# Sums moved into TensorE's waits around the last mix, the last pair stored as two halves, and one load moved to another queue

## The chip, the cores and the metric

The kernel runs on one core of one Trainium2 chip. The metric is the device time of one execution in microseconds (us), taken over several executions. A profile shows one execution; its times start with the first instruction of the core.

The engines: PE is TensorE (PEld its weight loads), DVE is VectorE, ACT is ScalarE, POOL is GpSimd, SP is SyncE. A "q" behind an engine's name is its sequencer, which issues DMAs. GpSimd issues the large loads, SyncE the stores.

## The reference, cut to what matters

A linear attention (8 batches, 8 heads, 576 positions, head size 64) makes `x`. Then comes a spectral mix:

```python
X = np.fft.rfft(x, axis=1)                       # [... 64 of the modes kept]
Yr = einsum(Xr, w_r) - einsum(Xi, w_i)           # 64 modes, each 512 x 512, two weight sets
Yi = einsum(Xr, w_i) + einsum(Xi, w_r)
y = np.fft.irfft(Y, n=S, axis=1)
u = x + y
return u + np.maximum(u @ w_ch, 0.0)             # float32, 8 x 576 x 512
```

The weights `w_r` and `w_i` are 64 x 512 x 512 floats each, 134 MB together. They are read once, and they are most of the 163.64 MB that the profile shows read from HBM.

## The kernel before: the parts that the change and the argument touch

The weights go through SBUF in tiles of 8 modes. A `mix` multiplies one tile with the spectrum; the last mixes finish the modes 48 to 63 ("late" modes). All other modes have been added to `x` (in `xs`) and to its product with `w_ch` (in `xw`) before. What is left after the last mix is, for every chunk of 128 output rows, two sums in PSUM, `p` (which is u) and `q` (which is u @ w_ch):

```python
class Last:                           # one item: one chunk, or a pair of chunks
    def base(self, which):            # which=0: p <- turned xs;   which=1: q <- turned xw
        ...                           # single first items and pairs take p from banks(): 2 buffers
    def late(self, which):            # adds the late modes: rows of yl (y for p, z for q)
        r = 64 * a + 32 * which
        back(..., CL, yl, slice(r, r + 16 if self.early else r + 32), not self.early)
    def straight(self, which):        # only the first chunks ("early"): last 8 modes from yst, zst
        pe.matmul(..., lhsT=CM[:, n], rhs=(yst, zst)[which], start=False, stop=True)
    def relu(self): ...               # ACT: relu of q, into rl
    def store(self): ...              # DVE: p + rl, then a DMA by SyncE
```

The late sums of later items read 32 rows of `yl`. The upper 16 of them are copies of the results of the very last mix: `yst` (y) and `zst` (y @ w_ch). Four DMAs make these copies; the second copy of `zst` is issued by GpSimd:

```python
def put(src, o, dst, copies):
    if o < 6:
        sp.dma_start(dst[16 * o:16 * o + 16], src)
    else:
        for s in copies:
            r = 32 * s + 16 * (o - 6)
            (sp, pool)[s // 2 if o == 7 else 0].dma_start(yl[r:r + 16], src)
```

Around the last mix:

```python
if not mixq:
    seq[0].base(1); seq[0].late(1)             # before the last mix
mix(...)                                       # waits for the last weights
seq[0].base(0); seq[0].late(0)
# yst = py + yacc (DVE), transposes (PE), yT (ACT, DVE)
seq[0].straight(0); seq[0].keep_p(); seq[1].base(1)
# pz = yT @ w_ch (PE), zst = pz (ACT, DVE), put(zst, ...)
seq[1].late(1); seq[1].base(0); seq[1].late(0)
seq[0].straight(1); ...                        # needs zst
for g, s in enumerate(seq):                    # t is the next item
    # t.base(1), s.base(0), t.late(1), s.late(0), t.relu(), s.store()   [cut]
```

## Time and profile before

| what | number | where it is read |
|---|---|---|
| time before | 452.13 us median of 3 runs (451.09 to 453.21) | timed runs |
| span of the profiled run | 450.4 us | page |
| last weight tile: issue to landing | 375.78 to 414.22 us | chain of waits |
| last mix starts | 414.26 us | timeline |
| from there to the end | 36.1 us | 450.4 - 414.26 |
| one pair of chunks in the tail | PE 1.30, ACT 1.08, DVE 1.22 us | timeline |

The page's strip of the DMA engines shows how busy they are in 40 slices of the span, in tenths (9 is 90% or more):

```profile
DMA  8999999999999999999999999999999999995597
```

They are 90% busy or more in 36 of 40 slices. Most of the kernel is a stream of weights, and the compute is arranged around it. The chain of waits of the last 40 us of before follows (start us, us, what):

```profile
375.78 38.44 DMA wt<-in_moe_w_i_dram
...
414.26 0.67 PE pt L37 x8
414.93 0.64 PE pp L37 x2
...
442.06 1.24 DVE of L37
...
443.38 0.60 ACT rl L37
...
444.50 1.22 DVE of L37
```

The stream ends at 414.22, 38 us after the issue of its last tile: that is how long the queue is. Between `414.93` and `442.06` the chain holds nothing but PE, apart from three pieces of 0.05 us or less (cut here). The timeline of before shows the steps that matter (start us, us, engine, operation, out<-in, count, and in brackets the idle time before and its releaser):

```profile
414.26 0.67 PE L37 MATMUL pt<-wt,XT 128*32 128x512 bf16 x8 [1.43 <-DMA wt<-in_moe_w_i_dram]
414.87 0.39 PE L37 MATMUL pp<-xs,CF 128*128 128x512 bf16 x1
415.19 0.39 PE L37 MATMUL pp<-yl,CL 16*128 16x512 bf16 x1
...
417.47 0.43 DVE L37 CAST zst<-pt 128x256 bf16<-128x256 f32 x1 [1.07 <-PE pt L37]
...
418.27 0.39 PE L37 MATMUL pp<-zst,CF 128*128 128x512 bf16 x1
418.50 0.54 POOL L37 DMA_DIRECT2D yl<-zst  x1 [1.60 <-DVE zst L37]
...
422.03 0.39 PE L37 MATMUL pt<-yl,CL 32*128 32x512 bf16 x2
...
422.35 0.61 PE L37 MATMUL pt<-xw,CF 128*128 128x512 bf16 x2
```

PE idles 1.43 us before the last mix. The base and late sum of the first chunk stand right after it (414.87, 415.19). GpSimd issues its copy of `zst` at 418.50. The view of issues gives 3.5 us from issue to landing for it, so it lands at 422.0. PE comes to the first late sums over 32 rows at 422.03 and finds them ready.

At the head, the timeline of before shows what releases PE:

```profile
2.85 0.75 POOL L37 DMA_DIRECT2D vn<-in_v_dram  x1
...
8.01 0.49 DVE L37 CAST w2blk<-xs 64x128 bf16<-64x128 f32 x2
...
8.23 1.12 PE L37 MATMUL one<-ident_b,kb 128*128 128x128 bf16 x9 [8.23 <-DVE w2blk L37]
...
9.14 1.30 PE L37 MATMUL one<-ident_b,qb 128*128 128x128 bf16 x10
...
10.38 1.89 PE L37 MATMUL two<-w2blk,kT 128*128 128x256 bf16 x8
```

GpSimd spends 0.75 us on the issue of v, and DVE's tables wait for what GpSimd does after it.

### The profile page before, as it was taken

How to read it: one execution, taken by the hardware profiler on the slowest of the kernel's cores; microseconds unless marked ns; L12 is line 12 of the kernel's file. 1: busy time of each engine (PE TensorE's matmuls, PEld its weight loads, DVE VectorE, ACT ScalarE, POOL GpSimd, SP SyncE). 2: the span in 40 equal slices, each digit the busy share in tenths (PEclk: the TensorE clock that was granted, in tenths of full speed). 3: DMA queues.
4: the chain of work that ended last, by engine and by line, in shares of the span. 5: the costliest groups of instructions: out<-in, count | busy, mean ns of one | idle time of the engine just before them, and what ended most of it. 6: DMA issues, size and time to landing. Idle time of an engine off the chain costs nothing.

```text
span 450.4 us, 9754 instructions
## 1 busy us (share of the span) xinstructions
PE 329.1 (73%) x4069; PEld 209.5 (47%) x4113; DVE 276.3 (61%) x519; ACT 274.6 (61%) x472; POOL 94.8 (21%) x128
## 2 busy tenths in 40 slices
PE   2577658669678767778768769208998677898994
PEld 2355546547456545566546646103554333343331
DVE  6667675655777567577676677664333233776685
ACT  3588868665898687598777675032433222664673
POOL 7142132123131222232321112401312120000000
PEclk9979988886999699699998989757999999999998
DMA  8999999999999999999999999999999999995597
GB/s 162 233 207 207 234 208 234 232 208 261 207 207 234 234 234 232 213 230 227 217 230 225 229 218 206 206 207 207 209 207 220 214 215 214 202 201 100 195 380 314
DMA packets 83981, 99.27 MB, mean 220 GB/s; under 512 B 2464, under 2 KB 79136, under 8 KB 83936
## 3 DMA queue, kind: packets, MB, share of 16 engines
q0 software_dynamic: 78192, 86.78, 108.5%
q1 hardware_dynamic: 5744, 11.86, 8.1%
q8 instruction: 32, 0.52, 0.4%
q14 instruction: 13, 0.11, 0.1%
HBM read 163.64 MB, written 9.44 MB: 384 GB/s over the span
## 4 chain that ended last, share of the span: by engine, by line
DMA 28%; PE 26%; issue 17%; ACT 12%; DVE 12%; POOL 5%; ACTq 0%; POOLq 0%; DVEq 0%
DMA wt<-in_moe_w_i_dram 13%; PE pt L37 11%; PE one L37 8%; DMA wt<-in_moe_w_r_dram 8%; DMA vn<-in_v_dram 6%; ACT AB L37 5%; PE two L37 4%; DVE m L37 3%; POOL wt L37 3%; ACT AQ L37 3%; PE pp L37 3%; DVE mk L37 2%; DVE zall L37 2%; DVE va L37 1%; DVE xs L37 1%
## 5 line engine op out<-in xcount | busy, mean ns | idle before, releaser
L37 ACT ACTIVATE AB<-two 128x1024 bf16<-128x1024 f32 x64 | 62.8, 1051 | 8.1 <-DVE mk L37 6.7
L37 ACT ACTIVATE AQ<-two 128x1024 bf16<-128x1024 f32 x64 | 63.2, 1059 | 2.6 <-PE two L37 2.6
L37 ACT CAST xw<-pt 128x512 bf16<-128x512 f32 x50 | 29.4, 588 | 43.2 <-PE pt L37 43.2
L37 PE MATMUL pt<-wchb,xT 128*128 128x512 bf16 x127 | 36.3, 398 | 22.4 <-DVE xT L37 20.8
L37 DVE TENSOR_REDUCE m<-two 128x8 f32<-128x1024 f32 x32 | 39.2, 1224 | 19.9 <-PE two L37 19.8
L37 DVE TENSOR_REDUCE mk<-two 128x8 f32<-128x1024 f32 x32 | 39.0, 1221 | 15.2 <-PE two L37 14.7
L37 DVE TENSOR_TENSOR va<-vn,ee 128x1152 bf16<-128x1152 f32 x32 | 42.0, 1355 | 3.4 <-DMA vn<-in_v_dram 3.4
L37 POOL DMA_DIRECT2D wt<-in_moe_w_r_dram x30 | 26.5, 885 | 78.8 <-PE pt L37 47.9
L37 POOL DMA_DIRECT2D wt<-in_moe_w_i_dram x28 | 24.8, 887 | 67.0 <-PE one L37 33.6
L37 DVE RECIPROCAL rd<-one 128x6 f32<-128x6 f32 x48 | 9.4, 196 | 47.1 <-PE one L37 47.1
L37 ACT COPY kT<-one 128x512 bf16<-128x512 bf16 (+1 forms) x32 | 19.1, 641 | 27.0 <-PE one L37 26.9
L37 PEld LDWEIGHTS <-minus 96*128 96x128 bf16 x288 | 26.2, 109 | 19.5 <-issue 13.3
L37 PE MATMUL two<-w2blk,qT 128*128 128x256 bf16 x128 | 21.9, 299 | 16.5 <-ACT AB L37 12.3
L37 PEld LDWEIGHTS <-XT 128*32 128x32 bf16 x512 | 18.3, 179 | 31.7 <-issue 18.0
L37 PEld LDWEIGHTS <-xs 128*128 128x128 bf16 x304 | 24.5, 99 | 15.1 <-issue 8.1
L37 PE MATMUL two<-mT,minus 96*128 96x128 bf16 x256 | 28.6, 241 | 3.0 <-issue 1.7
L37 PEld LDWEIGHTS <-qT 128*128 128x128 bf16 x144 | 14.5, 104 | 31.0 <-issue 27.9
L37 PEld LDWEIGHTS <-xT 128*128 128x128 bf16 x144 | 13.4, 102 | 32.0 <-DVE xT L37 20.5
L37 DVE TENSOR_TENSOR xs<-one,rd 128x384 bf16<-128x384 f32 x48 | 26.8, 557 | 1.6
L37 DVE COPY xT<-pt 128x512 bf16<-128x512 bf16 x36 | 15.2, 422 | 19.9 <-PE pt L37 19.9
L37 PE MATMUL pt<-wt,XT 128*32 128x512 bf16 x208 | 18.5, 431 | 11.4 <-DMA wt<-in_moe_w_i_dram 8.7
L37 PE MATMUL one<-kvz,AQ 128*128 128x65 bf16 x512 | 26.6, 206 | 0.1
(129 smaller groups left out, 695.0 us busy)
## 6 DMA issues: line engine op xcount, KB each, us to landing
wt<-in_moe_w_r_dram POOLq DMA_DIRECT2D x30, 1024.0 KB, 25.3
wt<-in_moe_w_i_dram POOLq DMA_DIRECT2D x28, 1024.0 KB, 24.7
vn<-in_v_dram POOLq DMA_DIRECT2D x16, 576.0 KB, 18.4
out_dram<-of SPq DMA_DIRECT2D x17, 512.0 KB, 3.6
kb<-in_k_dram POOLq DMA_DIRECT2D x16, 288.0 KB, 19.7
qb<-in_q_dram POOLq DMA_DIRECT2D x16, 288.0 KB, 18.3
xs<-in_moe_w_i_dram POOLq DMA_DIRECT2D x2, 1024.0 KB, 25.3
yacc<-in_moe_w_r_dram POOLq DMA_DIRECT2D x1, 1024.0 KB, 9.8
```

Of the source, the lines that this page charges most:

```text
L37: ins = f(*args, **kwargs)
```

## The change

The intent has three parts. (a) SyncE issues v of the first unit, so GpSimd gets to its other work sooner. (b) Sums of the first chunks move into waits of PE: the first chunk's `p` goes before the last mix, the second chunk's sums move up one place, and the third item's base of `q` goes into the wait for `zst`. (c) The last pair becomes two single chunks, so that its first half is stored earlier.

```diff
-        def load_v(self):
+        def load_v(self, eng=pool):
-            load(self.vn, v, self.g, self.bp, pool)
+            load(self.vn, v, self.g, self.bp, eng)
-    units[0].load_v()
+    units[0].load_v(sp)                                                     # (a)
-    seq += [Last(*x) for x in pairs[3]]
+    seq += [Last(*x) for x in pairs[3][:3]] + [Last((3, 6)), Last((3, 7))]  # (c)
             seq[0].late(1)                                                  # (b), to the end
+            seq[0].base(0)
+            seq[0].late(0)
         mix(*key, wts.pop(key), XTb[g % 2], bank)
             if end:
-                seq[0].base(0)
-                seq[0].late(0)
+                seq[1].base(1)
+                seq[1].late(1)
                 seq[0].keep_p()
-                seq[1].base(1)
+                seq[1].base(0)
-    seq[1].late(1)
-    seq[1].base(0)
     seq[1].late(0)
+    seq[2].base(1)
     seq[0].straight(1)
-        if t:
+        if t and g > 1:
             t.base(1)
```

(The comments are added here, and lines between the pieces are cut.)

## The prediction

> **What bounds the kernel now.** A stream of weights, then a tail. In the windows table the DMA share is 1.20 to 1.26 (16 engines) in nearly every stretch from 4 to 407 us. The chain of waits has a piece "DMA wt<-in_moe_w_i_dram" from 375.78 to 414.22 us: the last weight tile lands 38 us after its issue, because the queue is full. TensorE does the last mix at 414.26, and 36 us of tail follow (to 450.4), in which the chain is nearly all PE: one pair of output chunks every 1.30 us, while DVE needs 1.23, ACT 1.09, and stores run at about 400 GB/s (512 KB in 1.30 us).
>
> **What the change does.**
> (a) v of the first unit goes by SyncE. GpSimd issues what follows 0.75 us earlier (v's issue took that at 2.85), so DVE's w2blk (8.01 to 8.50, which releases TensorE at 8.23) comes about 0.7 us earlier. But compute at the head is not the bound. What counts is how early the DMA engines fill: their share is 0.2 to 0.6 between 2.0 and 4.0 us, over 1.0 afterwards. SyncE has issued w_phi by 1.97; w_phi landed 2.9 us after issue, so v can flow from about 3.1 and use half of 0.7 us. The Trainium skill (DMA: Bandwidth & Descriptors, "Issuing engines are not separate DMA queues") says that several issuers save only sequencer time and share 16 engines; the full shares in the trace agree. Estimate: the stream ends 0.3 us earlier (0 to 0.7).
>
> (b) The first chunk's base and late sum (0.64 us of PE, 414.87 to 415.5) move into the wait for the last weights (412.85 to 414.26), so they are free. The same sums of the second chunk take their place, so transposes, yT and zst keep their times. After pz one late sum and two base sums (0.32 + 0.43) replace three sums that ended at 418.27; the first straight sum of z then starts at 418.07, bound by DVE's zst (417.90). PE is 0.2 us ahead, and 0.65 us once the third item's base sums are skipped.
> Most is lost at once: the first late sum that reads all 32 rows (PE at 422.03) needs the GpSimd copy yl<-zst, issued at 418.50 and landing 3.5 us later, about 422.0. Before, PE arrived just then; now it arrives near 421.4 and waits some 0.5 us. From there PE has no slack, so the tail keeps its times; only the first pair's store leaves 0.65 us earlier.
>
> (c) The last pair in halves: DVE 0.69 + 0.69 instead of 1.22. The last DVE operation was 444.50 to 445.72; store data flowed without a gap from 443.2 to 448.4 at 400 GB/s, so the last bytes move little: 0 to 0.3 us.
>
> **Sum.** 0.3 (head) + 0.1 (mix) + 0.15 (halves), about 0.6 us. Predicted 451.5 us, range 449.9 to 452.9 (three runs of before spread over 2.1 us). Faster by over 2%: 1%; within 2%: 98%; slower: 1%.
>
> **What would show it.** The last wt lands near 413.9; TensorE's first matmul comes near 7.5, not 8.23; the first chunk's base and late sum stand before the mix, which still waits for the DMA; a new PE wait on yl before the first 32-row late sum, about 0.5 us; the distance from last mix to end is shorter by 0.1 to 0.4 us, not 0.65; the last store's data end close behind the one before.
>
> **What would make it wrong.** The copy of zst lands earlier than I read, so the whole 0.65 us comes through; 2 KB store rows are slower; v on the other queue delays kb past 7.5 us; run-to-run spread hides everything.

## The result

The changed kernel took 452.34 us in the median of 6 runs (451.91 to 452.95). Before took 453.12 in the same rounds (451.09 to 453.71, 6 runs). The ratio is 0.9991, with a 95% interval of 0.9970 to 1.0013: the same, to within what the runs can tell. (A ratio is the mean time of one kernel's fast runs over that of the other's of the same rounds, so it is not quite the ratio of the medians.) A second set of rounds, after_again, gave 1.0001 (0.9976 to 1.0025).

In the profile the last mix starts at 413.42, which is 0.84 us earlier than in before. The end comes at 450.1, only 0.3 earlier. So the tail became longer: 36.7 us instead of 36.1. Most of that lies behind the landing of the last store; the section on why takes it up.

The timeline of the changed kernel around the last mix:

```profile
412.06 0.39 PE L37 MATMUL pp<-xs,CF 128*128 128x512 bf16 x1
...
412.38 0.38 PE L37 MATMUL pp<-yl,CL 16*128 16x512 bf16 x1
...
413.42 0.68 PE L37 MATMUL pt<-wt,XT 128*32 128x512 bf16 x8 [0.65 <-DMA wt<-in_moe_w_i_dram]
...
416.64 0.43 DVE L37 CAST zst<-pt 128x256 bf16<-128x256 f32 x1 [1.07 <-PE pt L37]
...
417.24 0.38 PE L37 MATMUL pp<-zst,CF 128*128 128x512 bf16 x1
...
417.67 0.54 POOL L37 DMA_DIRECT2D yl<-zst  x1 [1.60 <-DVE zst L37]
...
420.56 0.39 PE L37 MATMUL pt<-yl,CL 32*128 32x512 bf16 x1
...
421.21 0.37 PE L37 MATMUL pt<-yl,CL 32*128 32x512 bf16 x1 [0.27 <-DMA yl<-zst]
```

It is best read as distances from the last mix, since the mix itself moves from run to run:

| step | before | changed |
|---|---|---|
| zst on DVE | 3.21 | 3.22 |
| first sum of z by PE | 4.01 | 3.82 |
| GpSimd issues the copy of zst | 4.24 | 4.25 |
| DVE's first sum of a pair (its store follows) | 7.93 | 7.30 |
| first late sum over 32 rows | 7.77 | 7.14 |
| next base sums, after both late sums | 8.09 | 8.10 |

PE gains 0.19 us at the first sum of z and has 0.63 us at the first late sum over 32 rows. The second late sum of that pair reads the rows that GpSimd copies. It waits for the DMA, and the sums behind it have the distance that they had before. Only the stores ahead of that wait leave earlier (the first chunks' by 0.19 us, the first pair's by 0.63). For the rest of the tail the gain is gone at that one wait. The chain of waits of the changed kernel, which in before is PE alone at this place, goes through the copy:

```profile
417.67 3.50 DMA yl<-zst
...
421.21 0.91 PE pt L37 x3
```

PE has one more wait in the tail. The view of waits, PE only, 412 to 451 us, of the changed kernel (for whom, us in total, times, longest):

```profile
PE pt L37 <- DMA wt<-in_moe_w_i_dram: 0.6, 1, 0.6
PE pp L37 <- DVE of L37: 0.4, 1, 0.4
PE pt L37 <- DMA yl<-zst: 0.3, 1, 0.3
```

The one in the middle is new as well. It comes from the split of the last pair, and experiment c_only takes it up.

At the head of the changed kernel, the timeline shows:

```profile
2.02 0.59 SPq L37 DMA_DIRECT2D vn<-in_v_dram  x1
...
7.26 0.49 DVE L37 CAST w2blk<-xs 64x128 bf16<-64x128 f32 x2
...
7.49 1.12 PE L37 MATMUL one<-ident_b,kb 128*128 128x128 bf16 x9 [7.49 <-DVE w2blk L37]
...
9.16 1.28 PE L37 MATMUL one<-ident_b,qb 128*128 128x128 bf16 x10 [0.56 <-DMA qb<-in_q_dram]
...
10.38 1.89 PE L37 MATMUL two<-w2blk,kT 128*128 128x256 bf16 x8
```

PE starts 0.74 us earlier, as intended. But q now lands 7.0 us after its issue instead of 5.3 (view of issues). By the landing records v is ahead of it now (v at 7.80, q at 9.11), while in before q was ahead of v (7.47 and 9.19). PE waits for q, and the first products start at 10.38 in both kernels. The compute of the head has gained nothing. Over all profiles below, q takes 6.9 to 7.4 us in the ten with v by SyncE, and 5.3, 5.5, 5.8 and 6.8 us in the four with v by GpSimd: a slow q occurs there too (c_only), so not every part of the delay need be due to v. The first products start at 10.36 to 10.38 us in the four, and at 10.31 to 10.76 (mean 10.57) in the ten.

### The profile page after: what moved, and what is told of

It reads as the page before. It is cut to its first block, busy times and chain, and to the rows that moved or that the text cites. A ratio compares the mean times of both kernels' runs of the same rounds, so it can differ in the third digit from the quotient of the medians.

```text
span 450.1 us, 9761 instructions
## 1 busy us (share of the span) xinstructions
PE 326.3 (72%) x4069; PEld 206.1 (46%) x4113; DVE 276.4 (61%) x520; ACT 274.6 (61%) x472; POOL 93.9 (21%) x127
## 4 chain that ended last, share of the span: by engine, by line
DMA 37%; PE 22%; ACT 18%; DVE 15%; issue 6%; POOL 1%; ACTq 0%; POOLq 0%; DVEq 0%
DMA wt<-in_moe_w_i_dram 15%; DMA wt<-in_moe_w_r_dram 14%; PE one L37 9%; ACT AB L37 6%; DVE m L37 6%; PE two L37 6%; DMA kb<-in_k_dram 6%; ACT AQ L37 5%; PE pt L37 5%; DVE mk L37 3%; ACT kT L37 2%; PE pp L37 2%; DVE zall L37 2%; DMA qb<-in_q_dram 2%; ACT qT L37 1%
## 5 line engine op out<-in xcount | busy, mean ns | idle before, releaser
L37 PE MATMUL pt<-wchb,xT 128*128 128x512 bf16 x127 | 37.6, 410 | 16.4 <-DVE xT L37 15.1
L37 PEld LDWEIGHTS <-minus 96*128 96x128 bf16 x288 | 24.9, 105 | 18.5 <-issue 11.7
L37 PE MATMUL two<-w2blk,qT 128*128 128x256 bf16 x128 | 20.9, 289 | 16.4 <-ACT AB L37 12.2
L37 PE MATMUL two<-mT,minus 96*128 96x128 bf16 x256 | 27.4, 234 | 2.5 <-issue 1.0
L37 PE MATMUL two<-w2blk,kT 128*128 128x256 bf16 x128 | 21.5, 297 | 6.4 <-ACT AB L37 6.4
L37 PE MATMUL one<-kvz,AQ 128*128 128x65 bf16 x512 | 25.5, 202 | 0.0
```

The source lines that it names most:

```text
L37: ins = f(*args, **kwargs)
```

## The experiments

All kernels gave the right result except the one that is wrong on purpose. There are two theories about the tail. Theory B: the tail is PE's chain, and the landing of GpSimd's copy of `zst` decides when that chain goes on. Its rival: the stores, at 400 GB/s, bound the tail by themselves, and PE's order does not matter. There are smaller questions about v (theory A) and about the split (theory C).

### a_only: v by SyncE alone

```diff
-    units[0].load_v()
+    units[0].load_v(sp)
```

> Only the first unit's v by SyncE; everything else as before. Theory A (the earlier start of the DMA engines and of GpSimd's issues carries through the full DMA queue): the last mix starts at about 413.4 us as in the changed kernel (before: 414.26), the tail from last mix to the end of the span stays at before's 36.1 us, time ratio about 0.998. Rival (the 0.84 us of the two profiles is run-to-run scatter of the weight stream): the last mix lands anywhere between 413 and 415.5 and the ratio is 1.000.

Measured: ratio 1.0013 (0.9992 to 1.0034), so no gain can be seen in the time. The last mix came at 412.98, which fits the theory; the rival, which allowed 413 to 415.5, is not excluded by it. The tail of this profile can't be compared: it lasted 40.5 us, and the view of windows shows why (columns: window, us, busy times of PE, PEld, DVE, ACT, POOL, then granted clock, DMA share, GB/s):

```profile
416.00:420.00 4.00, 4.00 (x13) 1.54 (x13) 0.44 (x2) 0.96 (x2) 0.59 (x2) 0.50 0.26 66
420.00:424.00 4.00, 4.00 (x13) 1.13 (x11) 1.38 (x2) 1.38 (x3) 0.00 (x0) 0.61 0.47 143
424.00:428.00 4.00, 4.00 (x25) 1.14 (x24) 2.29 (x2) 2.47 (x5) 0.00 (x0) 1.00 0.23 88
```

By the trace's clock records PE was granted half its clock for 10.24 us, from the last mix on. This run says nothing about the tail. The question of the head goes on below, under "All profiles together".

### b_only: the moved sums alone

The edit is part (b) of the diff, without (a) and (c).

> Only the first chunks' sums moved around the last mix. Theory B (the gain is lost at the wait for GpSimd's copy yl<-zst): TensorE waits about 0.3 us for yl<-zst, the base sums of the fifth item come 8.1 us after the last mix as in before, last mix to end stays at 36.1 us, ratio 1.000. Rival (the moved sums shorten the tail by PE work taken out, and the split of the last pair gave it back): last mix to end is 35.5 us, ratio 0.9986.

Measured: ratio 0.9987 (0.9969 to 1.0005). PE waits 0.2 us for yl<-zst. The first late sum over 32 rows is 7.15 us after the mix, the second 7.77, and PE's last sum 29.58 (before: 29.60). From the mix to the end it is 36.0 us (before: 36.1). The theory has it: the moved sums are faster up to the copy, and worth nothing behind it. (The 0.2 us are what is left of the wait after the first late sum, which doesn't need this copy.)

### c_only: the split of the last pair alone

```diff
-    seq += [Last(*x) for x in pairs[3]]
+    seq += [Last(*x) for x in pairs[3][:3]] + [Last((3, 6)), Last((3, 7))]
```

> Only the last pair as two halves. Theory C (three items with two PSUM double banks make the last base sum wait for VectorE's sum of the item two before, and the two halves take 1.37 us of VectorE instead of 1.22): TensorE waits about 0.4 us for VectorE of the pair before, last mix to end is 36.4 to 36.7 us, ratio 1.001. Rival (halves let the store start earlier): last mix to end 35.8 us, ratio 0.9993.

Measured: ratio 0.9995 (0.9978 to 1.0011). PE waits 0.4 us for DVE of an earlier item, as expected. The clock fell to half for 3.41 us in this profile too, just after the last mix, so that mix to end (37.8 us) can't be used. What the split costs at the end is seen better in the changed kernel itself (mix at 413.42). There PE's last sum is 30.53 us after the mix instead of 29.60, and DVE's last sum ends at 31.70 instead of 31.46 (445.12 against 445.72 on the clock of each run). The reason is in the code: `p` comes from two double banks of PSUM. With three items in a row where two were, the third needs the bank that DVE still reads.

Yet the end of the store stream hardly moved, as the section on the store stream shows.

### a_b: the change without the split

The edit is parts (a) and (b).

> The changed kernel without the split of the last pair. Theories A, B and C together: last mix at about 413.4, wait on yl<-zst 0.3 us, last mix to end 36.1 us (changed kernel: 36.6), so 0.5 us faster than the changed kernel, ratio to before 0.998. If the split was harmless: last mix to end 36.6 as in the changed kernel.

Measured: ratio 0.9978 (0.9958 to 0.9998). Last mix at 412.67, wait on yl<-zst 0.3 us, PE's last sum at 29.59, mix to end 36.2 us, against 36.7 in both profiles of the changed kernel. The 0.5 us came as expected, but not by the wait and the longer sums of the split: 0.43 us of it lie behind the landing of the last store (1.34 us from there to the end in the changed kernel, 0.91 here), and that landing differs by only 0.07 us (35.35 against 35.28 us after the mix). The section on why gives the cause.

### b_copy: the late copy by another queue

This was meant to take the wait away: ScalarE has just made half of `zst` and has time, so it issues the second copy.

```diff
-                (sp, pool)[s // 2 if o == 7 else 0].dma_start(yl[r:r + 16], src)
+                (sp, act if src is not yst else pool)[s // 2 if o == 7 else 0].dma_start(yl[r:r + 16], src)
```

> The changed kernel without the split, and the copy of the last zst that GpSimd issued goes out by ScalarE's queue, right after zst. Theory B (the copy's landing bounds the tail): the copy is issued 3.7 us after the last mix instead of 4.25 and lands about 7.0 us after it, TensorE (there at 7.4) no longer waits, the fifth item's base sums come 7.45 us after the last mix instead of 8.09, last mix to end is 35.5 us instead of 36.1, ratio to before about 0.9965. Rival (the stores at 400 GB/s bound the tail): TensorE is 0.6 us earlier, but the end stays 36.1 us after the last mix.

This failed. Measured: ratio 0.9985 (0.9956 to 1.0015), mix to end 36.6 us, PE's last sum 29.60, and the wait for yl<-zst still 0.3 us. The copy was issued 3.72 us after the mix, as meant, but it landed 4.0 us later, while GpSimd's took 3.5. The view of issues of b_copy (last number: us from issue to landing), 416 to 420 us:

```profile
yl<-zst SPq DMA_DIRECT2D x1, 128.0 KB, 3.2
yl<-zst ACTq DMA_DIRECT2D x1, 128.0 KB, 4.0
```

The same view of a_b:

```profile
yl<-zst SPq DMA_DIRECT2D x1, 128.0 KB, 3.3
yl<-zst POOLq DMA_DIRECT2D x1, 128.0 KB, 3.5
```

3.72 + 4.0 is 7.7, and 4.24 + 3.5 is 7.7. The landing did not move, and neither did PE's chain or the landing of the last store behind it (35.29 us after the mix, a_b 35.28). The Trainium skill (DMA: Bandwidth & Descriptors, "Issuing engine by pattern") calls the DMAs issued by SyncE and ScalarE "generally faster". For SyncE this trace agrees (3.2 to 3.3 us, beside 3.5 for GpSimd). ScalarE's copy took 4.0 us, here and in b_copy_split2, but it was issued only 12 ns after SyncE's, and GpSimd's comes 0.54 us after it. No run has a copy by ScalarE alone, so whether ScalarE or the crowding is slower is open.

### b_slow: the copy made later

The dose in the other direction: GpSimd issues both copies of the last `zst`, one after the other.

```diff
-                (sp, pool)[s // 2 if o == 7 else 0].dma_start(yl[r:r + 16], src)
+                (sp, pool)[(s // 2 if src is yst else 1) if o == 7 else 0].dma_start(yl[r:r + 16], src)
```

> The changed kernel without the split, and both copies of the last zst by GpSimd, the one that the 32-row sums need last being issued second. Theory B: that copy is issued about 0.55 us later and lands 8.3 us after the last mix, the wait for yl<-zst grows from 0.3 to about 0.85 us, last mix to end grows from 36.1 to 36.65. Rival (stores bound): the wait grows, but the end stays at 36.1.

Measured: PE waits twice for yl<-zst, 0.7 us together (0.3 in a_b). The second late sum comes 8.27 us after the mix instead of 7.77, and PE's last sum at 30.08 instead of 29.59, which is 0.49 later. That is theory B. Mix to end is 36.4 us, however, only 0.2 above a_b: the last store landed 0.18 us later (35.46 against 35.28), and two profiles of before differ by 0.13 there. The ratio is 0.9996 (0.9964 to 1.0028).

### before_again: the scatter

No edit.

> The kernel before once more, for the scatter. Theory A: last mix at 414.3, within 0.3. Rival (scatter): last mix elsewhere between 413 and 415.5. Last mix to end 36.1, ratio 1.000.

Measured: last mix at 412.94, so 1.3 us from where the first profile of before had it. The theory's figure of 0.3 us for the scatter is wrong. Ratio of the same kernel to itself: 1.0029 (0.9988 to 1.0070). No ratio here that differs from 1 by 0.2% means much by itself. PE's last sum comes 29.61 us after the mix (29.60 in the first profile): distances inside the tail repeat to 0.02 us where the clock does.

### b_copy_split2: halves without the PSUM wait

As b_copy, and the last pair stays a pair for PE; only its sum and its store are halved:

```diff
+            elif self.items[0] == (3, 6):
+                for a in range(2):
+                    dve.tensor_tensor(out=o[:, a], in0=self.p[a], in1=self.rl[:, a], op=ALU.add)
+                    sp.dma_start(...)          # 2 KB rows, one chunk
+                return
```

> As b_copy, and only the last sum and its store are halved: TensorE's order and PSUM of the last pair stay those of one pair. Theory C (it was the PSUM wait of the split that cost): no wait of TensorE for VectorE, the last sum of VectorE ends 0.3 us earlier than in b_copy, the end 0 to 0.3 us earlier. Rival (2 KB rows of the store cost time by themselves): the end comes later than in b_copy.

Measured: ratio 0.9991 (0.9959 to 1.0023). PE no longer waits for DVE, as theory C said. The clock fell for 3.41 us after the mix again, so only distances from PE's last sum (444.47) are used. The timeline, DVE only, has the last three sums in one line:

```profile
443.96 2.42 DVE L37 TENSOR_TENSOR of<-pp,rl 128x1024 f32<-128x1024 f32 x3
```

They end at 446.38, which is 1.91 us after PE's last sum; in b_copy the whole sum ends 1.86 after it. The expectation that the halves bring DVE's end forward by 0.3 us failed. Only the first half was ready early, at 1.31 us, and its store was issued at 1.81, against 1.88 for the whole store in b_copy: by the trace's records SyncE paused for 0.44 us before it, for a reason that no run shows. The last store landed 5.74 us after PE's last sum, and in b_copy 5.68. The halves bought nothing here, and the run does not test what an earlier half would bring.

### The store stream, read from all profiles

Whether the last store waits behind others can be seen in the DMA records. The following strips show the DMA engines in 40 slices of 0.05 us. In each fence the first line starts 28 us after the last mix, the second 33 us after it. Before (442.26 to 444.26, then 447.26 to 449.26):

```profile
DMA  9979999798989640112996987987987979899498
...
DMA  9989989898988898999989204001301000000000
```

The changed kernel (441.42 to 443.42, then 446.42 to 448.42):

```profile
DMA  9979999798999541110996987997989699698898
...
DMA  9899597795989969799997994220220220202000
```

In both there is a short gap 28.8 us after the mix, then a full stream without a gap until 34.2 to 34.3, then a few stragglers. The last four stores follow each other in it (2 MB at 400 GB/s). So PE's and DVE's delay by the split is hidden under the stream. From the end of the gap to the end of the full stream it is 5.29 to 5.37 us in all profiles but drop_store: 5.35 in the changed kernel, 5.36 in b_copy_split2 and 5.37 in c_only, against 5.29 to 5.32 without halves. Halving therefore costs about 0.05 us in the stream. (In steps of 10 ns: the gap begins and ends with the first and the last step with at most four packets in flight, and the stream ends with the first such step after it.)

The gap itself is the moment at which the stream had caught up with PE: the store before was through, and the first of these four was issued only 27.75 us after the mix. That is PE's pace. In b_slow it comes at 29.25, 0.47 later, and the stream ends at 34.73. So both theories hold a part. PE's chain sets when the last run of stores begins, and the store stream hides small delays of PE and DVE after that (how small, drop_store shows).

### drop_store: a wrong result on purpose

```diff
             rows = out[2 * bp + n // 4]
+            if (bp, n) == (3, 4):
+                return                          # the store of the last pair but one is left out
             sp.dma_start(
```

> Wrong result on purpose: the kernel a_b without the store of the last pair but one (512 KB missing). If the last stores queue behind each other (theory C: that is why the split's later TensorE and VectorE did not show), the last store starts as soon as it is issued, and its data end at 33.8 us after the last mix instead of 34.25. If VectorE's last sum alone set the end, the end stays at 34.25.

Measured (one look): the full stream now has a hole from 31.63 to 32.67 us after the mix, and the last store's data run from there to 34.07. That is 0.2 us earlier than with the store (34.23 in a_b), not 0.45 as expected. The last store did wait for the one before it, but only for 0.2 us. DVE's last sum at 31.44 is nearly as binding as the stream. So an earlier last store could by itself gain 0.2 us at most.

### b_fill: the wait for the copy filled

The fourth item's base sums of `p` go before its late sums, to where PE waits; nothing else changes against a_b:

```diff
         if g > 1:
-            s.base(0)
+            if g != 3:
+                s.base(0)
             if g == 2:
                 s.late(0)
                 s.straight(0)
+                t.base(0)
```

> The changed kernel without the split, and the fourth item's two base sums of p (0.43 us of TensorE) stand before its late sums, in the wait for yl<-zst. Theory B (the tail is TensorE's chain, and the wait for the copy ate the gain): no wait for yl<-zst, TensorE's last sum comes 29.15 us after the last mix instead of 29.59, the short gap of the store stream that was at 28.8 us after the mix in all unslowed runs comes at 28.35, and the stream's main part ends at 33.8 instead of 34.25; the end scatters by 0.3 us on top. Ratio to before about 0.997. Rival (the store stream alone bounds the tail): gap and end of the stream stay at 28.8 and 34.25.

Measured: ratio 0.9978 (0.9955 to 1.0000), 451.09 us in the median. The view of waits has none for yl<-zst. The timeline of b_fill (last mix at 413.27) shows why: PE does the base sums (the first line) and then meets the copy, which landed at 421.02, in the middle of the two late sums:

```profile
420.31 0.59 PE L37 MATMUL pp<-xs,CF 128*128 128x512 bf16 x2
420.84 0.60 PE L37 MATMUL pt<-yl,CL 32*128 32x512 bf16 x2
```

PE's last sum is 29.18 us after the mix (29.59 in a_b). The gap comes at 28.36, and the full stream ends at 33.84. Strips of b_fill with the same distances as above (441.27 to 443.27, then 446.27 to 448.27):

```profile
DMA  6999832101989969699699696999898969939969
...
DMA  9989989999998604003003004000000000000000
```

Gap and end both moved by 0.4 us, as theory B said to within 0.05. The rival falls: the store stream alone does not bound the tail. Mix to end is 35.8 us, the shortest of all; the last store landed at 34.86 (a_b: 35.28). The times alone would not show this: a_b has the same ratio, 0.9978, in its rounds.

### after_again and b_fill_again

No edits.

> The changed kernel once more, on the chip and in the rounds of b_fill. Theory: wait on yl<-zst 0.3 us, TensorE's wait for VectorE at the last half 0.4 us, TensorE's last sum 30.5 us after the last mix, gap of the store stream at 28.8 and main end at 34.3 as in before; ratio to before 0.999, b_fill faster than it by 0.4 us.

Measured: wait on yl<-zst 0.2 us, wait for DVE 0.4, PE's last sum 30.51, gap at 28.77, end of the full stream 34.30, mix to end 36.7: all as in the first profile of the changed kernel. In the same rounds b_fill's mean was about 1.0 us below this kernel's (0.9978 against 1.0001). The two traces have 0.9 us from mix to end, of which 0.47 come before the last landing and 0.42 behind it.

> The same kernel as b_fill in other rounds, for the scatter: gap of the store stream again at 28.36 us after the last mix, main end at 33.84, no wait for yl<-zst. Theory: 0.25 us from the head and 0.4 us from the tail make a ratio to before of 0.9986, so the 0.9978 of b_fill is in part scatter; if the 0.9978 is all effect, the ratio comes out there again.

Measured: ratio 0.9973 (0.9931 to 1.0015), median 450.94 us. Gap at 28.36 and end at 33.82, as expected. The ratio is again lower than the 0.9986 that the parts add up to, but its interval is wide and holds both. b_fill was faster than before in two sets of rounds, by 0.2 to 0.3% in the mean, though neither interval excludes 1; the traces account for 0.3 to 0.4 us of it in the tail.

### All profiles together

| kernel | v by | last mix | PE's last sum* | last store landed* | mix to end | ratio to before |
|---|---|---|---|---|---|---|
| before | GpSimd | 414.26 | 29.60 | 35.12 | 36.1 |  |
| before_again | GpSimd | 412.94 | 29.61 | 35.25 | 36.2 | 1.0029 |
| b_only | GpSimd | 414.05 | 29.58 | 35.00 | 36.0 | 0.9987 |
| c_only | GpSimd | 413.88 | clock fell | clock fell | 37.8 | 0.9995 |
| a_only | SyncE | 412.98 | clock fell | clock fell | 40.5 | 1.0013 |
| changed | SyncE | 413.42 | 30.53 | 35.35 | 36.7 | 0.9991 |
| after_again | SyncE | 413.45 | 30.51 | 35.33 | 36.7 | 1.0001 |
| a_b | SyncE | 412.67 | 29.59 | 35.28 | 36.2 | 0.9978 |
| b_copy | SyncE | 413.04 | 29.60 | 35.29 | 36.6 | 0.9985 |
| b_slow | SyncE | 412.81 | 30.08 | 35.46 | 36.4 | 0.9996 |
| b_copy_split2 | SyncE | 413.49 | clock fell | clock fell | 38.0 | 0.9991 |
| b_fill | SyncE | 413.27 | 29.18 | 34.86 | 35.8 | 0.9978 |
| b_fill_again | SyncE | 413.11 | 29.16 | 34.84 | 35.8 | 0.9973 |
| drop_store | SyncE | 413.04 | 29.59 | 34.84 | 35.8 | one look |

(* us after the last mix, to the start of PE's last matmul and to the end of the last store's DMA.)

For the head, the last mix comes at 413.78 in the mean of the four profiles with v by GpSimd, and at 413.13 in the mean of the ten with v by SyncE. That would be 0.65 us. But the four spread over 1.3 us, and most of the ten would fit among them. A steadier measure is how many bytes the DMA engines have moved by 40 us. Before, first 40 us:

```profile
DMA packets 7020, 8.06 MB, mean 202 GB/s; under 512 B 256, under 2 KB 6762, under 8 KB 7018
```

The changed kernel:

```profile
DMA packets 7182, 8.10 MB, mean 202 GB/s; under 512 B 255, under 2 KB 6796, under 8 KB 7180
```

The four profiles have 8.02 to 8.09 MB (mean 8.055) and the ten 8.06 to 8.13 (mean 8.09). The difference of 0.035 MB at 202 GB/s is 0.17 us. The DMA records have the same lead, 0.04 to 0.05 MB in the mean, at 100, 200, 300 and 400 us. So the stream is probably ahead by about 0.2 us with v on SyncE. That it is more than nothing in the final time is not shown.

## Why the prediction was right or wrong

The predicted time was 451.5 us, within 449.9 to 452.9, and "within 2%". Measured were 452.34 us and a ratio of 0.9991. The verdict and the range were right, and the expected gain of 0.6 us was not far from the 0.4 us of the first set of rounds; neither can be told from zero. That the sum came out near is luck: its part for the halves brought nothing, and the tail became longer instead of shorter.

- **What bounds the kernel: right.** The last mix waits for a weight tile whose DMA was issued 38 us before, in both kernels, and the tail behind it is PE's chain.
- **(a), the stream: probably right in mechanism, size open.** I estimated 0.3 us from the DMA share between 2 and 4 us. That share rose only from 0.54 to 0.61 between 3 and 4 us. The bytes say 0.17 us, the last mix 0.65 with a scatter as large, and the time of a_only nothing. I also named kb as the load that might suffer. It was q: it landed 1.7 us later after its issue and took back the 0.74 us that PE had gained at the start. The statement that the compute at the head is not the bound did not need it.
- **The skill's statement holds here.** The Trainium skill (DMA: Bandwidth & Descriptors, "Issuing engines are not separate DMA queues") says that several issuing engines save sequencer time and share the DMA engines. GpSimd's work came 0.74 us earlier, and q landed 1.7 us later after its issue.
- **(b), the wait for the copy: right, and the central point.** PE was 0.19 us ahead at the first sum of z (predicted 0.2) and 0.63 us ahead at the late sums (predicted 0.65). It then lost all of it at the copy. The idle time shown there is 0.3 us rather than 0.5: the first of the two late sums does not need that copy and ran at once, which hid a part. b_fill proved the point by filling the wait (PE's last sum 0.41 us earlier), and b_slow by lengthening it (0.49 us later).
- **(c), the halves: wrong.** The step that failed is "The last pair in halves: DVE 0.69 + 0.69 instead of 1.22 ... 0 to 0.3 us" gained. I costed DVE and the store, and did not ask where the third item's `p` would be: PE waited 0.4 us for a PSUM bank, its last sum came 0.9 us later and DVE's last sum 0.24 us later. The reason that I gave for a small effect, the nearly full write stream, was right, and it worked in the other direction too: it hid most of this loss (the last store landed at 35.35 and 35.33, in a_b at 35.28). In b_copy_split2, without the wait, DVE's two halves ended no earlier than the whole. The Trainium skill (Perfetto Trace Analysis, "DMA Optimizations") offers splitting where "DMA engines are generally idle"; here they were full for the 5.3 us of the last stores, and no run gained from it.
- **The tail from mix to end: wrong in sign.** I predicted it shorter by 0.1 to 0.4 us. It was 36.7 in both profiles of the changed kernel, against 36.1 and 36.2 of before. The full store stream ends at the same distance (34.3), and the last store lands 0.1 to 0.2 us later. Most of the rest, 0.37 us, comes after that landing: 1.34 us to the end of the span, against 0.98. The prediction had no term for this stretch. In it SyncE goes through one wait for each of eight DMA semaphores (the counters that tell of a landing), always in the same order and 0.06 us each. These records are in the view of the last line of the kernel (`--source`), from the landing on: the changed kernel, 448.77 to 449.29, then before, 449.39 to 449.55:

```profile
L931 SPq EVENT_SEMAPHORE  x8: 28/28/28, 448.8 to 449.2; - x8
...
L930 SPq EVENT_SEMAPHORE  x2: 28/28/28, 449.4 to 449.5; - x2
```

In the changed kernel the last store has the first of the eight semaphores, so all the other waits are still to be gone through when it lands; in before it has the last but one. Which one it has goes with the number of DMAs that SyncE and ScalarE issue in the whole program: 39 in before (two waits from the landing on), 40 in a_b and c_only (one), 41 in the changed kernel and in b_copy (eight), 42 in b_copy_split2 (seven). All 14 profiles fit, with 0.91 to 0.98 us after the landing for one or two waits and 1.28 to 1.35 for seven or eight. No run changes this count alone, but b_copy has the eight waits without the split, and c_only has the split without them. So this part of the loss comes neither from PE's and DVE's delay by the split nor from the store stream: v on SyncE and the second half's store are two more DMAs, and with them the last store has another semaphore.

## What to carry to other kernels

When you move work out of a chain, follow the chain to the next thing that it takes from elsewhere, and read when that lands: here PE was 0.63 us early at a DMA copy that had been just in time before, and all was lost there. What helps is to have other work ready for exactly that wait (b_fill), or a truly earlier landing; another queue that issues sooner but lands at the same time is no help. Before splitting the last store, see whether the store stream is already full and whether the extra item still has a buffer of its own. When two kernels' ends are compared, look at the landing of the last store as well as at the end of the span: here 0.37 us of difference came after it, from the order of waits.

## What the Trainium skill lacked or had wrong

- DMA: Bandwidth & Descriptors calls SyncE's and ScalarE's DMAs generally faster than GpSimd's. Copies of 128 KB from SBUF to SBUF beside another took 3.2 to 3.3 us from issue to landing by SyncE, 3.4 to 3.6 by GpSimd, and 4.0 by ScalarE (b_copy, b_copy_split2, issued 12 ns after SyncE's). GpSimd's first copy in b_slow, with none by SyncE, took 3.2. So for these copies the issuing engine alone does not say which is faster.
- DMA: Bandwidth & Descriptors says that issuing from several engines only saves issue time. It says that the DMAs interleave, but doesn't warn that a load moved forward on a second queue can delay one that is needed first: q landed 7.0 us after its issue instead of 5.3.
- TensorE: Matmul & The Clock Gate describes how the clock falls after idle time ("after ≥1 idle window (~3.4µs)", section "What's actually happening"). In 3 of 14 profiles the granted clock fell to 0.5 near the last mix, for 3.41, 3.41 and 10.24 us, though PE's waits for the last weights were 0.6 to 1.4 us there, and the records have PE busy for 60 to 79% of the 3.41 us before the fall; 11 profiles with waits of 0.1 to 1.4 us showed none. PE's last sum came 1.4 to 1.6 us and 4.3 us later with it. Each of the three profiled runs is the slowest of its kernel's six, so it is one source of the scatter between runs.
- No page says how far the same kernel's stream of loads scatters: the last tile of 99 MB landed 1.3 us apart in two profiles of one kernel.
- No page was found that tells what the order of the DMA semaphore waits at a kernel's end costs: 0.37 us between two kernels here, by the place of the last store's semaphore among eight.
